# A hand-ordered transformer block: the first part of its order table written anew, with w_phi third on the ACT queue and V of tile 0 between the last folds

## The chip, the core and the metric

The kernel runs on one core of a Trainium2 chip. The core has five engines with an instruction stream each: TensorE (PE, matrix products; its weight loads are shown as PEld), VectorE (DVE), ScalarE (ACT), GpSimd (POOL) and SyncE (SP), which here only issues DMAs. The engines wait for each other through semaphores. An engine takes its instructions strictly in the order in which they are written, so an instruction that waits holds up all that stand behind it. Loads and DMA transposes are issued from SP's queue, and a few loads from ACT's. The metric is the device time of one execution in microseconds, median of the runs. All times in profile rows are counted from the start of the profiled span.

## What is computed

One layer of linear attention with a learned feature map, and after it a gated feed-forward block, over 2048 rows of 640 values in bf16. Cut to what matters:

```python
# A: H = 32 heads of Dh = 20
xn = layernorm(x)
q, k, v = split_heads(xn @ wqkv)                    # wqkv: 640 x 1920
pq, pk = q @ w_phi[h], k @ w_phi[h]                 # w_phi: 32 x 20 x 20
phi(p) = concat(softmax(p), softmax(-p))
kv, z = phi(pk).T @ v, sum(phi(pk))
o = (phi(pq) @ kv) / (phi(pq) @ z + 1e-6)
h = x + o @ wo
# B: F = 1536
hn = layernorm(h)
out = h + ((hn @ w_gate) * (hn @ w_up)) @ w_down
```

## The kernel before

The 2048 rows are 16 tiles t of 128 rows; the 640 values are 5 chunks c of 128. In every name below, the number behind the letters is the tile or the chunk.

Because each head's key is multiplied by w_phi right after the projection, the kernel first folds w_phi into the key and query weights, so that later a single projection gives pk or pq. The steps at the start, with the names that the order table uses and the lines of the profile:

- loads (L285): `x0` ... `x14` are rows of x (one or two tiles each), `w5` is w_phi laid out over partitions (25 KB in runs of 40 bytes), `wk0` to `wk4` are the key weights by chunk, `wv0` to `wv4` the value weights by chunk, 160 KB each.
- `warm0` ... (L367, L372): products of zeros on PE that compute nothing.
- `WTc` (L392): PE transposes chunk c of the key weights; `WTec` (L251) copies the result from PSUM to SBUF. `Ph0` to `Ph2` (L380) spread w_phi into block form.
- `F1_c` (L411): the fold, six products that make chunk c of the folded key weights; `Fe1_c` (L251) copies it into place. `F0_c` and `Fe0_c` do the same for the query weights, whose transposes `wqtc` (L309) are done by DMA straight from HBM. Each `F0_c` reads all five `wqtc`.
- `L1st`, `L1at` (DVE, L428, L429, L431): mean and variance of tile t; `L1lt`, `L1et` (ACT, L436, L439): logarithm and exponential that make 1/sqrt; `L1nt` (L443): the bias for ACT's form; `xnt` (L453 on DVE, L451 on ACT): the normalized tile; `xtt` its transpose, on PE for tiles 0 and 1 (L462, copied by `xtet`), by DMA for the others (L471).
- `Vt`, `Kt`, `Qt` (L482): the projections, ten products of 128x320 each; for tiles 0 and 1 they are five separate steps of two products, one for each chunk, as in `V0_0` to `V0_4`, each of which needs its own chunk's weights only. `Vet` copies V; `Kxt_0`, `Kxt_1` (ACT, L494), `Kst` (DVE, L498), `Krt`, `Ket` (ACT, L501, L503) and `Knt` (POOL, L518) make phi of the keys; `KVt` (L526) adds the tile to kv and z. `Qxt`, `Qst`, `Qrt`, `Qbt` (a subtraction, L563), `Qet`, `Qnt` and the DMA transpose `qTt` (L575) do the like for the queries.
- After that come the division (`Nt`, `ddt`, `ot`), the output projection (`Ot`, L625), the second layernorm, the gated products (`U`, L668) and the last product (`D`, L687).

What sets the order is a table, `PLAN`: one entry for each step, with a key that it is sorted by, the choice among two engines where there is one, and the buffers (PSUM banks and SBUF slots) that it takes:

```python
PLAN[_f[0]] = (float(_f[1]), int(_f[2] or 0) if len(_f) > 2 else 0,
               tuple(int(_v) for _v in _f[3].split(",")) if len(_f) > 3 else ())
```

`arrange` sorts all steps by key and gives each engine its list; `emit` works out the waits. Nothing reorders at run time. So the table is each engine's program order, and the keys have no effect beyond it. The zero products `warm0` to `warm7` stand by dependence ahead of all PE transposes (`wall`).

Of the kernel before, what the change touches and what calls it, by code (L numbers as in the profile page):

```python
# [47 lines left out]
NFILL = 14  # L48
# [189 lines left out]
def build_graph():  # L238
    G = Graph()
# [130 lines left out]
    wm_b = Buf("pwarm", "psum")  # L370
    for k in range(8, 8 + NFILL):
        G.op("pe", "warm%d" % k, lambda e: e.matmul(pb(wm_b)[:, 0:256], lhsT=T["zero"][:, 0:P], rhs=T["zero"][:, :],  # L372
             start=True, stop=True), 0.11, LT, [z_b], [wm_b], -89, before=[G.by["warm%d" % j] for j in range(k)])
    wall = [G.by["warm%d" % k] for k in range(8)]
# [554 lines left out]
```

## Time and profile before

| | us |
|---|---|
| median of 3 runs | 272.42 |
| the three runs | 272.42, 272.93, 272.26 |
| span of the profiled execution, first to last instruction | 270.1 |
| what lies around the span (median less span) | 2.3 |
| PE busy in the span | 264.2 (98%) |
| DVE, ACT, POOL busy | 160.0 (59%), 124.0 (46%), 71.3 (26%) |

The profile page gives no time of its own for the profiled execution beside the span, so the 2.3 us are the median less that span. The busy share is an average over stages with different limits, and PE's products are pipelined, so the question in each stage is which wait ends last before PE can go on. Rows of the timeline give start, length, engine, line and tiles of a group of instructions, and in brackets how long the engine had been idle and what ended it.

### The profile page before, as it was taken

The page shows a single profiled execution, that of the slowest core. Times are in us where ns is not written, and L with a number is a line of the kernel's source. Part 1 is how long each engine was busy: PE and PEld are TensorE (multiplying, and loading weights), DVE is VectorE, ACT ScalarE, POOL GpSimd, SP SyncE. Part 2 cuts the span into 40 slices and gives each one's busy share as a digit, 9 for nine tenths or more (in the row PEclk, how much of TensorE's full clock was granted, in tenths as well). Part 3 has the DMA queues.
Part 4 walks back from the last instruction along what each step waited for, and adds up shares of the span by engine and source line. Part 5 has one row for each costly group of instructions (what it writes and reads, how often), then busy time and mean ns, then how long its engine had stood idle before and what let it go on. Part 6 is the DMA issues. An engine that isn't in the chain of part 4 may idle for free.

```text
span 270.1 us, 5186 instructions
## 1 busy us (share of the span) xinstructions
PE 264.2 (98%) x2092; PEld 177.9 (66%) x2105; DVE 160.0 (59%) x294; ACT 124.0 (46%) x316; POOL 71.3 (26%) x89
## 2 busy tenths in 40 slices
PE   7999999999999999999999999999999999999996
PEld 5777877777777788665556667765554476544774
DVE  4999799978988998577664253332342311423432
ACT  3899999988786382763540051222122300023000
POOL 4255689999923222205000000000000000000000
PEclk9999999999999999999999999999999999999999
DMA  7997995999958897973950001260200001100011
GB/s 200 318 168 136 249 222 129 302 183 245 204 106 143 163 126 149 140 123 64 171 93 2 0 0 36 57 106 1 73 12 2 0 0 51 49 1 0 27 49 61
DMA packets 71752, 28.09 MB, mean 104 GB/s; under 512 B 59056, under 2 KB 71728, under 8 KB 71728
## 3 DMA queue, kind: packets, MB, share of 16 engines
q1 hardware_dynamic: 71168, 27.10, 49.9%
q10 hardware_dynamic: 560, 0.66, 0.8%
q8 instruction: 16, 0.26, 0.4%
q14 instruction: 8, 0.07, 0.1%
HBM read 11.00 MB, written 2.62 MB: 50 GB/s over the span
## 4 chain that ended last, share of the span: by engine, by line
PE 90%; DMA 5%; DVE 2%; ACT 1%; issue 1%; SPq 1%; DVEq 0%
PE ps L668 36%; PE ps L482 24%; PE ps L687 19%; PE ps L625 6%; DMA scratch<-ph 2%; PE ps L526 2%; PE ps L588 2%; DMA Wp<-o 2%; DMA x_all<-in_A_x_dram 1%; PE ps L411 1%; SPq L653 1%; DVE st L428 0%; ACT Wp L251 0%; DVE st L429 0%; DVE ev L676 0%
## 5 line engine op out<-in xcount | busy, mean ns | idle before, releaser
L668 PE MATMUL ps<-xnT,Wgu 128*128 128x512 bf16 (+1 forms) x587 | 106.0, 335 | 0.7
L668 PEld LDWEIGHTS ps<-xnT,Wgu 128*128 128x128 bf16 x600 | 58.3, 98 | 43.4
L673 ACT ACTIVATE gt<-ps 128x512 bf16<-128x512 f32 (+1 forms) x60 | 29.7, 509 | 100.9 <-PE ps L668 62.9
L482 PE MATMUL ps<-Wp,xnT 128*128 128x320 bf16 (+1 forms) x480 | 68.6, 298 | 0.0
L482 PEld LDWEIGHTS ps<-Wp,xnT 128*128 128x128 bf16 x480 | 45.5, 97 | 17.2 <-issue 0.2
L676 DVE TENSOR_TENSOR ev<-ps,gt 128x512 bf16<-128x512 f32 (+1 forms) x60 | 33.6, 579 | 36.5 <-PE ps L668 27.8
L687 PE MATMUL ps<-Wd,ev 128*128 128x320 bf16 (+2 forms) x396 | 53.9, 295 | 0.0
L687 PEld LDWEIGHTS ps<-Wd,ev 128*128 128x128 bf16 x396 | 38.1, 98 | 15.3 <-DVE ev L676 0.2
L699 DVE SCALAR_TENSOR_TENSOR Wp<-ps,rs,x_all 128x640 bf16<-128x640 f32 (+3 forms) x18 | 14.6, 810 | 49.3 <-PE ps L687 49.1
L518 POOL TENSOR_TENSOR ek<-ek,SR 128x1280 bf16<-128x1280 bf16 x16 | 37.5, 2358 | 5.2 <-ACT SR L503 5.1
L551 ACT ACTIVATE ph<-ps 128x600 bf16<-128x600 f32 x32 | 21.4, 680 | 8.0 <-PE ps L482 6.9
L556 DVE TENSOR_REDUCE S<-ph 128x66 f32<-128x1320 bf16 x16 | 23.9, 1516 | 1.8 <-ACT ph L553 1.8
L625 PE MATMUL ps<-Wo,Wp 128*128 128x320 bf16 x160 | 23.9, 299 | 0.2
L498 DVE TENSOR_REDUCE SR<-ek 128x64 f32<-128x1280 bf16 x16 | 23.3, 1468 | 1.0 <-ACT ek L494 1.0
L570 POOL TENSOR_TENSOR ph<-ph,RQ 128x660 bf16<-128x660 bf16 x16 | 20.7, 1308 | 8.9 <-ACT RQ L566 8.9
L646 POOL TENSOR_SCALAR ln<-mv 128x1 f32<-128x1 f32 x12 | 2.3, 191 | 75.7 <-ACT ek L642 75.1
L494 ACT ACTIVATE ek<-ps 128x640 bf16<-128x640 f32 x32 | 21.2, 719 | 2.2 <-PE ps L482 1.5
L625 PEld LDWEIGHTS ps<-Wo,Wp 128*128 128x128 bf16 x160 | 15.3, 98 | 6.4 <-DMA Wp<-o 0.4
L631 DVE SCALAR_TENSOR_TENSOR x_all<-ps,x_all 128x640 bf16<-128x640 f32 x16 | 13.1, 821 | 6.4 <-PE ps L625 6.4
L615 DVE TENSOR_TENSOR o<-ps,sm 128x660 bf16<-128x660 f32 x16 | 13.4, 840 | 0.9 <-ACT sm L608 0.6
L642 ACT ACTIVATE ek<-x_all,mv 128x640 bf16<-128x640 bf16 x16 | 13.1, 821 | 0.0
L251 ACT ACTIVATE ev<-ps 128x640 bf16<-128x640 f32 x16 | 11.2, 704 | 1.1 <-PE ps L482 1.1
(69 smaller groups left out, 161.9 us busy)
## 6 DMA issues: line engine op xcount, KB each, us to landing
out_dram<-Wp SPq DMA_DIRECT2D x15, 160.0 KB, 1.8
Wgu<-in_B_w_gate_dram SPq DMA_DIRECT2D x4, 480.0 KB, 6.2
Wd<-in_B_w_down_dram SPq DMA_DIRECT2D x4, 480.0 KB, 4.7
Wgu<-in_B_w_up_dram SPq DMA_DIRECT2D x4, 480.0 KB, 5.6
x_all<-in_A_x_dram SPq DMA_DIRECT2D x5, 320.0 KB, 5.0
Wp<-in_A_wqkv_dram SPq DMA_DIRECT2D x5, 160.0 KB, 4.7
ev<-in_A_wqkv_dram SPq DMA_DIRECT2D x4, 160.0 KB, 4.2
x_all<-in_A_x_dram SPq DMA_DIRECT2D x3, 160.0 KB, 3.2
```

Of the source, the lines that this page charges most:

```text
L482: ins = e.matmul(pb(b, hb)[:, 0:n1 - n0], lhsT=T["xnT"][:, NC - 1 - c, P * t:P * (t + 1)], rhs=T["Wp"][:, POS[kind], c, n0:n1], start=(c = ...
L494: G.op("act", "%sx%d_%d" % (nm, t, s), lambda e, s=s, b=b, ek=ek: e.activation(out=T["ek"][:, ek.slots[0], 0:2 * D].rearrange("p (b h s f) ...
L498: G.op("dve", "%ss%d" % (nm, t), lambda e, ek=ek, sr=sr: e.tensor_reduce(out=T["SR"][:, sr.slots[0], 0, :], in_=T["ek"][:, ek.slots[0], 0: ...
L518: G.op("pool", "Kn%d" % t, lambda e, eng, ek=ek, sr=sr: e.tensor_tensor(out=T["ek"][:, ek.slots[0], 0:2 * D].rearrange("p (h f) -> p h f", ...
L551: e.activation(out=v[:, 0:10].rearrange("p (b g) j f -> p b g j f", b=2), in_=pp(b, 0, 300).rearrange("p b (g j f) -> p b g j f", j=3, f=D ...
L556: G.op("dve", "Qs%d" % t, lambda e, t=t, ph=ph: e.tensor_reduce(out=T["S"][:, t, 0:66].rearrange("p (g k) -> p g k", k=6), in_=pv(ph).rear ...
L570: return e.tensor_tensor(out=v, in0=v, in1=T["RQ"][:, rq.slots[0], 1, 0:33].rearrange("p (g j) -> p g j", j=3).unsqueeze(3).to_broadcast([ ...
L625: ins = e.matmul(pb(b, hb)[:, 0:320], lhsT=T["oT"][:, oT.slots[0], c, :], rhs=T["Wo"][:, c, 320 * hb:320 * (hb + 1)], start=(c == 0), stop ...
L668: ins = e.matmul(pb(b)[:, 0:n], lhsT=T["Wgu"][:, gu, c, P * ft:P * (ft + 1)], rhs=T["xnT"][:, NC - 1 - c, o0:o0 + n], start=(c == 0), stop ...
L673: G.op("act", "g%d_%d" % (bi, ft), lambda e, pg=pg, gt=gt, n=n: e.activation(out=T["gt"][:, gt.slots[0], 0:n], in_=pb(pg)[:, 0:n], func=AF ...
L676: o_ = G.op("dve", "u%d_%d" % (bi, ft), lambda e, pu=pu, gt=gt, hh=hh, ft=ft, n=n: e.tensor_tensor(out=T["hh"][:, hh.slots[0], ft, 0:n], i ...
L687: ins = e.matmul(pb(b, hb)[:, 0:w], lhsT=T["hh"][:, hh.slots[0], ft, P * tt:P * (tt + 1)], rhs=T["Wd"][:, ft, c0 + w * hb:c0 + w * (hb + 1 ...
```

## The change

The order table is written anew for the first part of the program; from about 75 us on the order is the old one. The keys are whole numbers now, places in the order. The table is 22 lines shorter, so a line L482 of the kernel before is L460 of the changed one, and so for all lines below the table. What it does:

- SP's and ACT's first loads: ACT issues `x0`, `wk1`, `w5` (before: `x1`, `wk3`); SP issues `x1`, `x3`, `wk2`, `wk3`, `wk4`, `wk0`, `x4`, `wv0`, `wv1`, `wv2`, `wv4`, `wv3`, `x2`, `x6`, `x8` (before, with `x0`, `x3`, `w5` ahead: `wk0`, `wk4`, `wk1`, `wk2`, `x4`, `wv1`, `wv0`, `wv2`, `wv3`, `x2`, `wv4`, `x6`). The load `x12` moves from ACT to SP.
- PE: 20 zero products in place of 22, with at least sixteen ahead of any transpose (in the table seventeen, before eighteen); the key weights are transposed in the order 1, 2, 3, 4, 0 and folded in the order 1, 2, 0, 3, 4; `V0_0` to `V0_3` stand between the folds.
- DVE and ACT: DVE takes the statistics of tile 0 first, then `xn0`, `Ph1` (before on POOL), `xn1`; some copies out of PSUM, normalizing steps and bias steps change engine; on POOL the fills of constants come in another order; the subtractions `Qb2`, `Qb4` and `Qb9` move from DVE to POOL.
- SP's DMA transposes between 9 and 27 us come in another order, and `x10` is issued among them.

The few lines of code, with the table's first entries that bear on them:

```diff
-NFILL = 14
+NFILL = 12
...
-    wall = [G.by["warm%d" % k] for k in range(8)]
+    wall = [G.by["warm%d" % k] for k in range(16)]
```

PE's order at the start: before, from the first transpose of the key weights (L392; L372 are zero products, L462 is the transpose of a normalized tile, L411 a fold).

```order
3 L392 MATMUL ps<-ident,ev 128x128 x5
4 L372 MATMUL ps<-ev 128x256 x3
5 L392 MATMUL ps<-ident,ev 128x128 x5
6 L462 MATMUL ps<-ident,xn 128x128 x5
7 L392 MATMUL ps<-ident,ev 128x128 x10
8 L372 MATMUL ps<-ev 128x256
9 L411 MATMUL ps<-Phi,scratch 128x140 x2
```

And in the changed kernel (L370 transposes of the key weights, L350 zero products, L440 transposes of normalized tiles, L389 folds, L460 projections).

```order
3 L370 MATMUL ps<-ident,ev 128x128 x5
4 L350 MATMUL ps<-ev 128x256 x3
5 L370 MATMUL ps<-ident,ev 128x128 x10
6 L440 MATMUL ps<-ident,xn 128x128 x5
7 L370 MATMUL ps<-ident,ev 128x128 x5
8 L440 MATMUL ps<-ident,xn 128x128 x5
9 L389 MATMUL ps<-Phi,scratch 128x140 x2
10 L389 MATMUL ps<-Phi,scratch 128x80 x2
11 L389 MATMUL ps<-Phi,scratch 128x140 x2
12 L370 MATMUL ps<-ident,ev 128x128 x5
13 L460 MATMUL ps<-Wp,xnT 128x320 x2
14 L389 MATMUL ps<-Phi,scratch 128x140 x2
```

Before, two folds ran ahead of the second normalized tile's transpose; now only one fold stands ahead of the first projection step `V0_0` (the L460 row), and both normalized tiles are transposed before the first fold. The other four folds come behind it, with `V0_1` to `V0_3` between them.

SP's queue, before: from the load `x6` to the DMA transposes of tiles 6 and 7 (L471 transposes a normalized tile, L309 a chunk of the query weights).

```order
8 L285 DMA x_all<-in_A_x_dram 128x2x640
9 L471 DMA_TRANSPOSE xnT<-xn 128x5x128
10 L285 DMA x_all<-in_A_x_dram 128x2x640
11 L309 DMA_TRANSPOSE scratch<-in_A_wqkv_dram 128x1x640 x2
12 L471 DMA_TRANSPOSE xnT<-xn 128x5x128
13 L309 DMA_TRANSPOSE scratch<-in_A_wqkv_dram 128x1x640
14 L471 DMA_TRANSPOSE xnT<-xn 128x5x128
15 L309 DMA_TRANSPOSE scratch<-in_A_wqkv_dram 128x1x640
16 L471 DMA_TRANSPOSE xnT<-xn 128x5x128
17 L309 DMA_TRANSPOSE scratch<-in_A_wqkv_dram 128x1x640
18 L471 DMA_TRANSPOSE xnT<-xn 128x5x128 x2
```

And in the changed kernel (L449 transposes a normalized tile, L287 a chunk of the query weights).

```order
6 L263 DMA x_all<-in_A_x_dram 128x2x640 x2
7 L449 DMA_TRANSPOSE xnT<-xn 128x5x128
8 L287 DMA_TRANSPOSE scratch<-in_A_wqkv_dram 128x1x640
9 L263 DMA x_all<-in_A_x_dram 128x2x640
10 L449 DMA_TRANSPOSE xnT<-xn 128x5x128
11 L287 DMA_TRANSPOSE scratch<-in_A_wqkv_dram 128x1x640 x2
12 L449 DMA_TRANSPOSE xnT<-xn 128x5x128
13 L287 DMA_TRANSPOSE scratch<-in_A_wqkv_dram 128x1x640 x2
14 L449 DMA_TRANSPOSE xnT<-xn 128x5x128 x3
15 L263 DMA x_all<-in_A_x_dram 128x2x640 x2
```

The entries are, before: `x6`, `xt3`, `x8`, `wqt4` and `wqt1`, `xt5`, `wqt0`, `xt2`, `wqt2`, `xt4`, `wqt3`, `xt6` and `xt7`; now: `x6` and `x8`, `xt3`, `wqt0`, `x10`, `xt5`, `wqt2` and `wqt3`, `xt2`, `wqt4` and `wqt1`, `xt4`, `xt6` and `xt7`, `x12` and `x14`. Two loads of x share this stretch, all five query-weight transposes stand ahead of `xt4`, and eight transposes follow `xt5`, where seven did.

ACT's list at its start, before (L436 and L439 make 1/sqrt, L251 are copies out of PSUM).

```order
2 L285 DMA x_all<-in_A_x_dram 128x640
3 L285 DMA ev<-in_A_wqkv_dram 128x640
4 L436 ACTIVATE ln<-mv,eps 128x1
5 L439 ACTIVATE rs<-ln 128x1
6 L251 ACTIVATE scratch<-ps 128x5x128
7 L436 ACTIVATE ln<-mv,eps 128x1 x2
8 L439 ACTIVATE rs<-ln 128x1 x2
9 L251 ACTIVATE xnT<-ps 128x5x128
10 L251 ACTIVATE scratch<-ps 128x5x128
11 L251 ACTIVATE Wp<-ps 128x640 x5
```

And in the changed kernel (L414 and L417 make 1/sqrt, L229 are copies out of PSUM).

```order
2 L263 DMA x_all<-in_A_x_dram 128x640
3 L263 DMA ev<-in_A_wqkv_dram 128x640
4 L263 DMA w<-in_A_w_phi_dram 128x5x20
5 L414 ACTIVATE ln<-mv,eps 128x1
6 L417 ACTIVATE rs<-ln 128x1
7 L414 ACTIVATE ln<-mv,eps 128x1
8 L229 ACTIVATE scratch<-ps 128x5x128
9 L417 ACTIVATE rs<-ln 128x1
10 L414 ACTIVATE ln<-mv,eps 128x1
11 L417 ACTIVATE rs<-ln 128x1
12 L229 ACTIVATE scratch<-ps 128x5x128 x2
13 L229 ACTIVATE Wp<-ps 128x640 x4
```

Before, tile 1's logarithm and exponential stood next to each other at the head; now tile 0's come first, and between the logarithm and the exponential of tile 1 stands a copy of transposed key weights (`WTe1`).

More of the change, by code (lines that the diff above doesn't have):

```diff
@@ new lines @@
+id1:21 wk4:22:1 warm8:23::0 warm9:24 glb:25 wk0:26:1 warm10:27 ekz:28 warm11:29 x4:30 warm12:31 L1s0:32 warm13:33 warm14:34 wv0:35:1 warm15:36 warm16:37
+L1a0:38 wv1:39 L1s1:40 WT1:41::3 L1l0:42 warm17:43 wv2:44:1 L1e0:45 warm18:46 warm19:47 L1s3:48 wv4:49:1 wv3:50 Ph2:51 L1a1:52 xn0:53::3 WT2:54::5 x2:55
+L1l1:56 Ph0:57 WTe1:58:1 L1a3:59 WT3:60::0 Ph1:61:1 x6:62 xt0:63::1 L1e1:64 L1l3:65 WT4:66::4 xn1:67::0 x8:68 L1e3:69 WTe4:70 WTe3:71 xt1:72::2 xte0:73:1
+F1_1:74::6 WTe2:75 xte1:76:1 WT0:77::3 Fe1_1:78 WTe0:79:1 V0_0:80::4 F1_2:81::0 L1n3:82:1 xn3:83::2 V0_1:84 Fe1_2:85:1 F1_0:86::2 L1s5:87 xt3:88 V0_2:89
```

158 lines of the change are left out of this document (66 added, 92 removed).

## The prediction

> **What bounds the kernel now.** I read the page first, then the busy time by stage, then the chain of waits, and last the timeline of each engine up to 27 us, where the order changes.
>
> ```profile
> PE 264.2 (98%) x2092; PEld 177.9 (66%) x2105; DVE 160.0 (59%) x294; ACT 124.0 (46%) x316; POOL 71.3 (26%) x89
> ...
> PEclk9999999999999999999999999999999999999999
> ```
>
> ```profile
> 10.50:82.40 71.90, 71.90 (x738) 53.86 (x735) 64.89 (x100) 64.16 (x175) 51.88 (x45) 1.00 0.96 196
> 82.40:130.00 47.60, 46.77 (x408) 33.75 (x407) 38.60 (x79) 25.19 (x72) 12.91 (x20) 1.00 0.82 129
> ```
>
> The columns behind the stretch are its length and the busy time of PE, PEld, DVE, ACT and POOL. From 10.5 us PE has work without a gap for 71.90 us, and in the 47.60 us after it idles 0.83. So two things set the time: how much useful work PE has done when the dense stretch begins, and whether a new wait opens in it. Useful work on PE is the same in both kernels.
>
> ```profile
> 0.83 3.06 DMA x_all<-in_A_x_dram
> ...
> 10.70 14.95 PE ps L482 x110
> 25.65 0.64 PE ps L411 x12
> ```
>
> In the chain of waits the first load of x is what everything waits for, then DVE, ACT and the last fold; from 10.70 it is PE alone. 110 products of a projection take 14.95 us, 0.136 each, so a two-product step such as V0_0 is 0.27.
>
> ```profile
> 1.12 1.89 PE L367 MATMUL ps<-ev 128*128 128x256 bf16 x8 [1.12 <-DVE ev L365]
> ...
> 5.30 0.49 PE L372 MATMUL ps<-ev 128*128 128x256 bf16 x3
> 6.49 0.45 PE L392 MATMUL ps<-ident,ev 128*128 128x128 bf16 x5 [0.70 <-DMA ev<-in_A_wqkv_dram]
> 7.08 0.45 PE L462 MATMUL ps<-ident,xn 128*128 128x128 bf16 x5
> 7.37 0.72 PE L392 MATMUL ps<-ident,ev 128*128 128x128 bf16 x10
> 7.93 0.27 PE L372 MATMUL ps<-ev 128*128 128x256 bf16 x1
> 8.04 0.80 PE L411 MATMUL ps<-Phi,scratch 128*128 128x140 bf16 x12
> 8.68 0.44 PE L392 MATMUL ps<-ident,ev 128*128 128x128 bf16 x5
> 8.95 0.44 PE L462 MATMUL ps<-ident,xn 128*128 128x128 bf16 x5
> ...
> 10.54 15.11 PE L482 MATMUL ps<-Wp,xnT 128*128 128x320 bf16 x110
> ```
>
> PE's timeline gives the steps, start to start: a transpose of a tile 0.29 (7.08 to 7.37), a fold 0.32 (two from 8.04 to 8.68), a transpose of weights 0.27 (8.68 to 8.95). At 10.54 all five weight transposes, both tile transposes and five folds are behind PE.
>
> **The new start, step by step.** The second tile's transpose now stands ahead of every fold, so the question is when xn1 is there.
>
> ```profile
> 3.91 0.49 DVE L428 BATCH_NORM_STATS2 st<-x_all 128x6 f32<-128x320 bf16 x1 [2.85 <-DMA x_all<-in_A_x_dram]
> ...
> 5.50 0.19 DVE L431 BATCH_NORM_AGGREGATE mv<-st 128x2 f32<-128x12 f32 x1
> 5.61 0.44 DVE L428 BATCH_NORM_STATS2 st<-x_all 128x6 f32<-128x320 bf16 x1
> ...
> 6.47 0.55 DVE L453 TENSOR_SCALAR xn<-x_all,mv,rs 128x640 bf16<-128x640 bf16 x1
> ...
> 7.05 0.44 DVE L251 COPY scratch<-ps 128x640 bf16<-128x640 bf16 x1
> 7.59 0.61 DVE L453 TENSOR_SCALAR xn<-x_all,mv,rs 128x640 bf16<-128x640 bf16 x1
> ```
>
> ```profile
> 5.73 0.29 ACT L436 ACTIVATE ln<-mv,eps 128x1 f32<-128x1 f32 x1 [3.65 <-DVE mv L431]
> 6.06 0.20 ACT L439 ACTIVATE rs<-ln 128x1 f32<-128x1 f32 x1
> 6.17 0.69 ACT L251 ACTIVATE scratch<-ps 128x640 bf16<-128x640 bf16 x1
> 6.75 0.72 ACT L436 ACTIVATE ln<-mv,eps 128x1 f32<-128x1 f32 x2
> ```
>
> x0 is now ACT's first load, as x1 was, so DVE starts at 3.91 again. A tile's statistics take 0.80 (3.91 to 5.50 is two), an aggregate 0.11 (5.50 to 5.61). The new order has tile 0, aggregate, tiles 1 and 3, aggregate: tile 1's begins at 3.91 + 3 x 0.80 + 0.11 = 6.42. Its logarithm follows 0.23 behind (5.50 to 5.73), at 6.65. Behind it on ACT now stands a weight copy, and only then the exponential. The copy can start some 0.2 later (my estimate; one that waits for the logarithm starts after 0.33, 5.73 to 6.06), holds ACT for 0.58 (6.17 to 6.75), and the exponential takes 0.20: 7.63. The subtraction takes 0.61, to 8.27; PE follows 0.06 later (7.02 to 7.08), at 8.33. Tile 0's products are then long done, and Ph1 on DVE fits into the wait.
>
> From 8.33 PE goes through transpose, fold F1_1 and transpose WT0: 8.33 + 0.29 + 0.32 + 0.27 = 9.21. V0_0 also needs wv0.
>
> ```profile
> 4.65 1.90 SPq L285 DMA_DIRECT2D Wp<-in_A_wqkv_dram  x4
> ...
> 9.14 1.31 SPq L471 DMA_TRANSPOSE xnT<-xn  x1
> ...
> 11.11 3.44 SPq L309 DMA_TRANSPOSE scratch<-in_A_wqkv_dram  x2
> 14.59 1.28 SPq L471 DMA_TRANSPOSE xnT<-xn  x1
> ...
> 21.17 1.27 SPq L309 DMA_TRANSPOSE scratch<-in_A_wqkv_dram  x1
> 22.49 2.60 SPq L471 DMA_TRANSPOSE xnT<-xn  x2
> ```
>
> In the view of DMA issues, with the us from issue to landing, w_phi and the first value load stand so:
>
> ```profile
> w<-in_A_w_phi_dram SPq DMA_DIRECT2D x1, 25.0 KB, 4.3
> ...
> Wp<-in_A_wqkv_dram SPq DMA_DIRECT2D x1, 160.0 KB, 4.8
> ```
>
> The first value load, issued at 4.65, lands 4.8 later, at 9.45. It was wv1; now wv0 has that place, with the same loads ahead of it on the two queues together, so V0_0 starts at 9.5. Four V steps (1.09) and the other four folds (1.28) bring PE to 11.87, where the kernel before would stand at 10.54 + 1.09 = 11.63. **Term 1: +0.25.** Without the wait for wv0 it would be -0.05.
>
> V0_1 to V0_3 need the next value loads, half a microsecond apart (four issues in 1.90), and come at steps of about 0.6, wv3 with a place later: margins of 0.1 to 0.4, where before V began 2 us behind its loads. One place later costs 0.47. **Term 2: +0.1**, between 0 and 0.6.
>
> **The query folds.** 94 projection products follow, 94 x 0.136 = 12.78: F0_2's turn is at 11.97 + 12.78 = 24.75. It needs all five query-weight transposes; the last of them is now the sixth of a row that starts with tile 5's. That place was 14.59 to 21.17 before, 6.58 for five issues.
>
> Four of SP's transposes, each alone in its stretch of the view of DMA issues, with the us from issue to landing: tile 3's (issued at 9.14), a query chunk's (21.17), the one issued right behind tile 5's, and tile 4's.
>
> ```profile
> xnT<-xn SPq DMA_TRANSPOSE x1, 5.5
> ...
> scratch<-in_A_wqkv_dram SPq DMA_TRANSPOSE x1, 3.2
> ...
> scratch<-in_A_wqkv_dram SPq DMA_TRANSPOSE x1, 5.0
> ...
> xnT<-xn SPq DMA_TRANSPOSE x1, 2.8
> ```
>
> When does tile 5's come? WTe0 starts 0.56 behind WT0 (6.49 to 7.05), so at 9.50, and with xn3 behind it (0.44, a bias step, 0.60) tile 3's transpose is issued at 10.8, not 9.14. Behind it a query-weight transpose (1.27, or 2.17 where it was the second of the 3.44) and x10 (about 0.6): 14.1 to 15.0. I take 14.8. The last query transpose is issued at 21.4 and lands 3.2 later, 24.6, just in time; tile 4's, now behind it, lands at 22.7 + 2.8 = 25.5, where V4's turn is 24.75 + 0.64 = 25.4; V6 is as close. Before, tile 4's was issued one place ahead of the last query transpose, at 21.17 - 1.31 = 19.86. The margins are gone: 0 at best, and with a landing of 5.0, which one of the five had, 1.7. Nearest is the low end, with x10's 320 KB in line as well. **Term 3: +0.5.**
>
> The rest costs nothing: the two zero products fall in PE's idle time (0.70 at 6.49); the three subtractions go to POOL, which has 20 us free in the dense stretch (71.90 - 51.88); x12 comes later, as x10 did before, for which DVE waited 1.3 us (the second of the two below) while PE stayed dense. ACT begins the key features later, but it has 7.7 us free in that stretch (71.90 - 64.16); if these don't suffice, PE waits for PSUM.
>
> ```profile
> DVE st L428 <- DMA x_all<-in_A_x_dram: 4.2, 2, 2.9
> ```
>
> Sum: +0.85, span 270.1 + 0.85 = 270.9, and with the 2.3 around it, which make the span the median of 272.4: **273.3 us.**
>
> **The clock.** The profile shows the full clock in all 40 slices. Yet the first eight zero products took 0.24 each, those at 5.30 0.16. From the end of these at 5.8 PE ran only transposes until 7.93; now it does until the first fold at 8.62, 2.8 us against 2.1. [...]
>
> **Rivals.**
> 1. *Not slower.* PE's V steps fill the waits: wv0 lands early (-0.05), tile 5's transpose at 14.1, and the 0.83 us of idle time behind 82 us takes up part of what is left. Time 272.0 to 272.7. For it: every term is small. Against: xn1 is reached through DVE and ACT alone, so earlier loads of weights gain 0.3 at most. Faster by 0.8 would need nearly all the idle time that PE has from 10.5 to 130 us.
> 2. *SP's transposes come late.* Term 3 at its high end: F0_2 waits 1.7, and V4 and V6 behind it; 272.4 + 0.25 + 0.1 + 2 = 274.8. For it: tile 3's transpose took 5.5 to land and one query transpose 5.0. Against: the 5.0 ran beside x12 on ACT's queue, which is gone there.
> 3. *w_phi on ACT's queue lands late*, so that the change does not bring it early at all: Ph1 stands ahead of xn1 on DVE, so past 7.3 us each microsecond is paid in full. At 8.3: 274.3. Before, as third on SP's queue (issues about half a microsecond apart from 0.8) and 4.3 from issue to landing, it was there at about 6; third on ACT's that leaves 1.3.
> [...]
>
> **How the numbers follow.** A measurement of this kernel tells about 0.3%, 0.8 us, from no change (its runs differ by 0.67). My forecast, 272.9 to 274.0: 0.47. Rival 1: 0.24; rival 2: 0.14; rival 3: 0.08; rival 4: 0.04; something else 0.03. Slower by over 0.3% is above 273.24: 0.28 of the forecast's 0.47 and rivals 2 to 4, together 0.54. Faster needs the low end of rival 1: 0.07. Within: 0.39. The range of 8 in 10, with rival 1's middle and rival 2: 272.2 to 275.0.
>
> **What would show it.** Right: xn1's transpose on PE near 8.3, the 94 products from near 11.9, PE idle before L389 or L460 near 25 us with a DMA transpose as releaser. Wrong: PE's first V step well ahead of 9.5 (term 1), no wait at 25 (term 3), or a wait at 30 to 75 us for ACT or POOL, which would be the features' late start.

## The result

| | us |
|---|---|
| before, median of 6 runs | 272.41 |
| changed, median of 6 runs (274.60 to 276.92) | 275.45 |
| ratio, 95% interval | 1.0122 (1.0097 to 1.0147) |
| spans of the two profiled executions | 270.1 and 273.3 |

The changed kernel is slower by 1.2%, 3.0 us, where 0.85 was predicted. A second measurement of the same kernel, against the kernel before beside it, gave 1.0103 (1.0072 to 1.0133).

### The profile page after: what moved, and what is told of

It reads as the page before. It is cut to its first block, busy times and chain, and to the rows that moved or that the text cites. A ratio compares the mean times of both kernels' runs of the same rounds, so it can differ in the third digit from the quotient of the medians.

```text
span 273.3 us, 5182 instructions
## 1 busy us (share of the span) xinstructions
PE 265.4 (97%) x2090; PEld 177.9 (65%) x2103; DVE 159.1 (58%) x296; ACT 122.5 (45%) x314; POOL 71.0 (26%) x89
## 4 chain that ended last, share of the span: by engine, by line
PE 75%; DVE 10%; DMA 8%; ACT 4%; POOL 1%; issue 1%; SPq 0%; DVEq 0%
PE ps L646 36%; PE ps L665 19%; PE ps L460 10%; PE ps L603 7%; DMA Wp<-o 3%; DMA x_all<-in_A_x_dram 3%; DVE SR L476 2%; DVE st L407 2%; DMA xnT<-xn 2%; PE ps L566 2%; DVE st L406 2%; DVE xn L431 2%; ACT ek L472 1%; PE ps L504 1%; POOL ek L496 1%; ACT ph L529 1%
## 5 line engine op out<-in xcount | busy, mean ns | idle before, releaser
L460 PE MATMUL ps<-Wp,xnT 128*128 128x320 bf16 (+1 forms) x480 | 69.1, 299 | 0.9 <-DMA xnT<-xn 0.9
L460 PEld LDWEIGHTS ps<-Wp,xnT 128*128 128x128 bf16 x480 | 45.2, 97 | 18.6 <-DMA xnT<-xn 1.4
L677 DVE SCALAR_TENSOR_TENSOR Wp<-ps,rs,x_all 128x640 bf16<-128x640 f32 (+3 forms) x18 | 14.6, 810 | 49.3 <-PE ps L665 49.1
L603 PE MATMUL ps<-Wo,Wp 128*128 128x320 bf16 x160 | 23.9, 299 | 1.6 <-DMA Wp<-o 1.5
L603 PEld LDWEIGHTS ps<-Wo,Wp 128*128 128x128 bf16 x160 | 15.2, 98 | 8.3 <-DMA Wp<-o 2.4
L229 ACT ACTIVATE ev<-ps 128x640 bf16<-128x640 f32 x14 | 9.8, 706 | 2.3 <-PE ps L460 2.2
```

Of the source, the lines that this page charges most:

```text
L460: ins = e.matmul(pb(b, hb)[:, 0:n1 - n0], lhsT=T["xnT"][:, NC - 1 - c, P * t:P * (t + 1)], rhs=T["Wp"][:, POS[kind], c, n0:n1], start=(c = ...
L603: ins = e.matmul(pb(b, hb)[:, 0:320], lhsT=T["oT"][:, oT.slots[0], c, :], rhs=T["Wo"][:, c, 320 * hb:320 * (hb + 1)], start=(c == 0), stop ...
```

## The profile after

First the page of the changed kernel, then its windows with the boundaries of before (length, then busy time of PE, PEld, DVE, ACT, POOL, the granted clock, the DMA share, GB/s).

```profile
PE 265.4 (97%) x2090; PEld 177.9 (65%) x2103; DVE 159.1 (58%) x296; ACT 122.5 (45%) x314; POOL 71.0 (26%) x89
...
q8 instruction: 16, 0.26, 0.4%
```

```profile
10.50:82.40 71.90, 70.64 (x717) 52.56 (x715) 62.13 (x98) 62.16 (x168) 52.78 (x48) 1.00 0.88 189
82.40:130.00 47.60, 45.82 (x418) 33.14 (x419) 38.65 (x77) 26.22 (x76) 12.49 (x19) 1.00 0.76 127
```

The dense stretch is dense no longer: PE idles 1.26 us in it (71.90 less 70.64) where it idled nothing, and 1.78 behind it where it idled 0.83. The clock is 1.00 in both. Where the idle time lies, PE's timeline of the changed kernel shows (L440 is the transpose of a normalized tile, L389 a fold, L460 a projection, L504 the products of KV, L566 those of N, L603 those of O).

```profile
8.60 0.46 PE L440 MATMUL ps<-ident,xn 128*128 128x128 bf16 x5 [0.45 <-DVE xn L431]
...
9.21 0.44 PE L370 MATMUL ps<-ident,ev 128*128 128x128 bf16 x5
9.64 0.43 PE L460 MATMUL ps<-Wp,xnT 128*128 128x320 bf16 x2
...
11.73 12.99 PE L460 MATMUL ps<-Wp,xnT 128*128 128x320 bf16 x94
25.08 0.80 PE L389 MATMUL ps<-Phi,scratch 128*128 128x140 bf16 x12 [0.36 <-issue]
...
46.87 0.49 PE L504 MATMUL ps<-ev,ek 128*128 128x63 bf16 x11
...
47.75 6.41 PE L460 MATMUL ps<-Wp,xnT 128*128 128x300 bf16 x46
55.07 4.26 PE L460 MATMUL ps<-Wp,xnT 128*128 128x320 bf16 x30 [0.90 <-DMA xnT<-xn]
59.17 0.49 PE L504 MATMUL ps<-ev,ek 128*128 128x63 bf16 x11
...
114.84 0.50 PE L566 MATMUL ps<-KVm,scratch 128*128 128x63 bf16 x11
...
118.20 2.89 PE L603 MATMUL ps<-Wo,Wp 128*128 128x320 bf16 x20 [1.22 <-DMA Wp<-o]
```

The rows of PE's timeline before that stand for the same steps: KV7, KV8 and N15.

```profile
45.80 0.49 PE L526 MATMUL ps<-ev,ek 128*128 128x63 bf16 x11
...
57.02 0.49 PE L526 MATMUL ps<-ev,ek 128*128 128x63 bf16 x11
...
113.00 0.51 PE L588 MATMUL ps<-KVm,scratch 128*128 128x63 bf16 x11 [0.44 <-DMA scratch<-ph]
```

Step against step, PE is 1.07 us late at KV7 (46.87 less 45.80): the start. At KV8 it is 2.15 late; between the two lies V13, which waits for a DMA transpose of a normalized tile. At N15 it is 1.84 late, since the wait that the kernel before has there (0.44) is gone. Then O6 waits 1.22, and the span ends 3.2 later. So there are three places: the start, V13 and O6. (The steps ahead of KV7, KV8, N15 and O6 on PE are the same ones in both kernels, only in another order, so the rows compare equal work.)

The prediction looked at the first. For the second, SP's timeline of the changed kernel (L449 is a tile's transpose, L263 a load, L553 a query tile's transpose) and DVE's around it:

```profile
42.58 1.20 SPq L449 DMA_TRANSPOSE xnT<-xn  x1
43.82 2.32 SPq L263 DMA_DIRECT2D Wgu<-in_B_w_up_dram  x4
50.17 1.20 SPq L449 DMA_TRANSPOSE xnT<-xn  x1
```

```profile
48.15 1.48 DVE L476 TENSOR_REDUCE SR<-ek 128x64 f32<-128x1280 bf16 x1
49.55 0.60 DVE L431 TENSOR_SCALAR xn<-x_all,mv,rs 128x640 bf16<-128x640 bf16 x1
```

and SP's of the kernel before:

```profile
42.15 3.84 SPq L471 DMA_TRANSPOSE xnT<-xn  x3
46.04 2.30 SPq L285 DMA_DIRECT2D Wgu<-in_B_w_up_dram  x4
```

The transpose at 50.17 is tile 13's, `xt13`. Before, it was the first of the three at 42.15, ahead of the four 480 KB loads `wu2`, `wu3`, `wu0`, `wu1`. The new table puts `xn13` behind `Ks11` on DVE (the two DVE rows), so it ends 8 us later, and `xt13` behind the four loads. The chain of waits of the changed kernel has both late waits as pieces (start, length):

```profile
50.17 4.85 DMA xnT<-xn
...
113.52 4.64 DMA Wp<-o
```

## Tile 13: six runs

The question is whether tile 13's place causes the second loss, and by what: the loads ahead of its transpose (theory A) or the late subtraction by itself (rival D). The entries are a name, its key, and slots; nothing else of the table is touched.

**Both put back early** (in the changed kernel):

```diff
-xn13:338::3  xt13:341
+xn13:290.5::3  xt13:296.5
```

> The changed kernel, with only tile 13's subtraction (xn13) and its transpose (xt13) put back to the place that they have in the kernel before: xn13 ahead of xn15 on DVE, xt13 ahead of xt15 on SP. Theory A (queue): the changed kernel's second loss, 1.3 us at V13 (55.07 us), comes from xt13 standing behind four 480 KB loads, and PE's lateness then passes through SP's row of transposes (77 to 125 us) to the end, the wait of 1.22 at O6 with it. Then V13 doesn't wait, PE is about 1 us later than in the kernel before from 40 us to the end, and the time is 273.3 to 273.8. Rival B: the wait at O6 has a cause of its own (oT6 took 4.6 us to land, 3.8 before) and stays: 274.2 to 274.6. Rival C: what is gained at V13 is lost at the next wait, since something else sets the end: 275.2 to 275.6.

Measured: ratio 1.0051 (1.0027 to 1.0075), 273.36 us against 271.80 beside it. PE's timeline of this run has no wait from KV7 to KV8:

```profile
47.40 11.04 PE L460 MATMUL ps<-Wp,xnT 128*128 128x300 bf16 x80
58.28 0.50 PE L504 MATMUL ps<-ev,ek 128*128 128x63 bf16 x11
```

Neither V13 nor O6 waits; the span is 1.0 longer than before's. A's number came, B's and C's did not: about half of the loss goes with this one tile.

**Only the subtraction early**, twice (`xn13:290.5`, `xt13` still behind the loads):

> The changed kernel, with only the subtraction xn13 put back early (ahead of xn15 on DVE); its transpose xt13 stays behind the four loads on SP. Theory A (queue): xt13 is issued at about 46.2, right behind wu1, but lands only behind it (52.4), at 53.7 to 55.0; V13 waits 0.1 to 1.4; time 274.0 to 275.5. Rival D (late subtraction): xt13 lands 2.6 to 3 us from its issue, at about 49, V13 doesn't wait, time 273.3 to 273.8.

> The kernel with only xn13 early, a second time: xt13 still behind the four loads on SP. Is its time (ratio 1.0036) a matter of xn13's place, or of the one profiled execution in which the instruction fetch came 0.1 us after xt13's packets? If of xn13's place: xt13 lands again about 0.7 us behind wu1, V13 waits under 0.4, ratio 1.003 to 1.007. If of the fetch's chance: the fetch hits wu1 or xt13 this time, xt13 lands 1.5 to 2 us later against wu0's landing (4 in place of 2.1), V13 waits 0.5 to 1.5, and the ratio lies towards 1.010.

Measured: ratios 1.0036 (1.0014 to 1.0057) and 1.0065 (1.0038 to 1.0092); no wait at V13 in either profile, though `xt13` took 6.9 and 6.8 us from issue to landing behind the loads (SP's timeline of the first, where the issue itself took 2.96 us, and the row in its view of DMA issues):

```profile
47.48 2.96 SPq L449 DMA_TRANSPOSE xnT<-xn  x1
```

```profile
xnT<-xn SPq DMA_TRANSPOSE x1, 6.9
```

So where `xt13` stands in SP's queue need not matter; when `xn13` is done does. In both profiles PE came late from the start (1.9 and 2.6 us at KV7), which helps to hide it.

**One place earlier**, ahead of `Ks11` (`xn13:330.5`), with a start as late as the changed kernel's:

> The changed kernel with xn13 one place earlier on DVE, ahead of Ks11 in place of behind it (1.5 us): xt13 is issued at 48.5 to 48.8, not 50.1, and stands behind the four loads on SP, whose last lands at 52.4 to 54.3. If it is enough that xt13 is issued before the loads are through (it moves right behind them): V13 waits 0 to 0.6, ratio 1.004 to 1.008. If the subtraction must come 8 us earlier: V13 waits 0.9 to 1.8 as in the changed kernel, ratio 1.009 to 1.013.

Measured: ratio 1.0044 (1.0019 to 1.0069). SP's and PE's timelines:

```profile
48.65 1.20 SPq L449 DMA_TRANSPOSE xnT<-xn  x1
```

```profile
47.07 11.05 PE L460 MATMUL ps<-Wp,xnT 128*128 128x300 bf16 x80
57.95 0.50 PE L504 MATMUL ps<-ev,ek 128*128 128x63 bf16 x11
```

`xt13` is issued 1.52 us earlier, lands 4.3 later, at 53.0, and V13 doesn't wait: one place on DVE is enough.

**The loads behind xt13** (the changed kernel; `xn13` late):

```diff
-wu2:303 wu3:304 wu0:309 wu1:316
+wu2:341.1 wu3:341.2 wu0:341.3 wu1:341.4
```

> The changed kernel, with the four loads wu2, wu3, wu0, wu1 put behind xt13 on SP's queue; the subtraction xn13 stays late, behind Ks11. Theory A (queue): xt13 is issued at 50.2 as in the changed kernel, but lands about 2.6 later, at 52.8, ahead of V13's turn at 53.6; no wait there, time 273.3 to 273.8, as with xn13 and xt13 both early. Rival D (late subtraction): that xn13 ends at 50.15 rather than 42.1 is enough by itself; xt13 lands near 55 again, V13 waits some 1.3, time 275.2 to 275.6.

Measured: ratio 1.0281 (1.0235 to 1.0328); both theories missed the time. PE's and SP's timelines, and the transpose in the view of DMA issues:

```profile
54.33 4.26 PE L460 MATMUL ps<-Wp,xnT 128*128 128x320 bf16 x30 [0.49 <-DMA xnT<-xn]
```

```profile
51.10 3.44 SPq L263 DMA_DIRECT2D Wgu<-in_B_w_up_dram  x4
54.58 4.63 SPq L553 DMA_TRANSPOSE scratch<-ph  x1
```

```profile
q8 instruction: 1, 0.02, 3.4%
...
xnT<-xn SPq DMA_TRANSPOSE x1, 4.4
```

With no load ahead of it `xt13` still takes 4.4 us, and V13 still waits (PE loses 0.67 between KV7 and KV8). So A, as a story of the queue alone, falls. One rival is left open here: the four loads are issued at 51.10, right behind `xt13`, and move beside it. The time is worse for another reason: `qT1`, now behind the loads, lands 7.4 us after its issue, the next query tile waits for its buffer, and PE idles 3.0 us ahead of 65.01. And in five of the six runs the mean granted clock was 0.988 to 0.994, not 1.00 as in the profiled one, which is the fastest (277.08 of a median of 279.77).

**The converse**, the kernel before with `xn13` behind `Ks11` and `xt13` behind `wu1`:

> The converse: the kernel before, with xn13 moved behind Ks11 on DVE and xt13 behind wu1 on SP, as they stand in the changed kernel. Theory A (queue): in the kernel before the last of the four loads lands at 56.15; with xt13 out of the row ahead of them at about 55; xt13 lands 1.3 to 2.6 behind, at 56.3 to 57.6, and V13, whose turn is 52.8, waits 3.5 to 4.8. Nothing gives it back: 275.9 to 277.2. Rival D (late subtraction): xn13 ends near 48.6, xt13 lands at 51 to 52, no wait, 272.2 to 272.7. Rival C (another thing sets the end): a wait at V13, but less than 1 us of it left at the end, under 273.4.

Measured: ratio 1.0105 (1.0064 to 1.0145). PE's timeline:

```profile
55.73 4.26 PE L482 MATMUL ps<-Wp,xnT 128*128 128x320 bf16 x30 [2.07 <-DMA xnT<-xn]
```

The wait appears in the old kernel too, 2.24 us between KV7 and KV8, and stays to the end (the span is 2.6 longer). A had its place right and its size too high; D expected no wait and C no lasting loss, and fell.

The table gives, for each profile, how late the rows of KV7, KV8 and N15 start against those of the kernel before, and the span against 270.1.

| kernel | KV7 | KV8 | gained between | N15 | span |
|---|---|---|---|---|---|
| changed | 1.07 | 2.15 | 1.08 | 1.84 | 3.2 |
| changed, second profile | 0.74 | 2.49 | 1.75 | 2.52 | 3.2 |
| before, tile 13 late | 0.57 | 2.81 | 2.24 | 2.65 | 2.6 |
| loads behind | 0.74 | 1.41 | 0.67 | 4.28 | 5.3 |
| both early | 1.26 | 1.26 | 0 | 1.07 | 1.0 |
| subtraction early | 1.89 | 1.90 | 0 | 1.29 | 1.2 |
| subtraction early, again | 2.57 | 2.57 | 0 | 2.44 | 3.2 |
| one place earlier | 0.93 | 0.93 | 0 | 0.11 | 0.1 |

In all seven profiles with `xn13` late (three more below) PE loses 0.67 to 2.33 us between the two rows. (In the one with 2.33, `oT6` one place earlier, 0.60 of it is a wait for ACT at V9.) In all nine profiles of a changed kernel with `xn13` earlier it loses nothing.

## The instruction fetch: two runs

Why does a transpose that takes 2.6 us elsewhere (`xt15`, 42.58, in the same trace) take 4.4 to 5.3 at this place? The DMA view of the changed kernel for 52.0 to 54.5 (40 slices; then the queues, with packets, MB and their share of 16 engines):

```profile
GB/s 217 406 98 156 254 75 16 0 0 0 0 0 0 0 0 131 0 0 0 0 8 8 57 123 193 201 209 221 176 188 160 90 45 25 184 156 20 8 12 8
...
q14 instruction: 1, 0.01, 3.0%
q8 instruction: 1, 0.02, 2.9%
```

For about 0.8 us, from 52.45 to 53.25, no data packet starts. What is there are two instruction fetches: the one on queue 8 takes 2.9% of 16 engines over 2.5 us, 1.16 us of one engine. Sixteen of them come in a span (the page), one for about 260 of PE's 4193 instructions; that they bring PE's code was the author's guess from this ratio. That gave theory E, and two runs: the changed kernel once more, and one meant to move the fetches by 24 more narrow zero products at the start, which PE has idle time for (its first sixteen are narrower, too):

```diff
-NFILL = 12
+NFILL = 36
+WN = lambda k: 128 if k < 16 else 64 if k < 40 else 256
```

> The changed kernel, unchanged, on the chip of the next three. Theory E, formed from the traces so far: V13's wait is made by an instruction fetch (16 KB on queue 8, which comes at 52 to 54 us in every trace, with another of 8 KB on queue 14 near it) that holds one of the 16 DMA engines for 1.1 us just when the packets of xt13's transpose are moved; that happens because xn13 is done, and xt13 issued, 8 us later than before. The fetch goes with PE's place in its program, so V13 waits again, 0.9 to 1.5 us, and the time is 1.0% to 1.4% above the kernel before. Rival F (chance): the 4.9 us that xt13 took to land are an accident of the one profiled execution; this profile shows no wait at V13 and a span near 272.

> The changed kernel with 24 more zero products on PE (48 of PE's instructions, 64 columns each; the first 16 are cut to 128 columns, so that all end before the first weights land). Nothing else moves; only every later fetch of PE's code comes 48 instructions earlier in the work, some 2 to 3 us, at 49 to 50.5 us in place of 52.1. Theory E: xt13, issued at about 50.2 as in the changed kernel, is through behind the last of the four loads (52.4) at 53.0 to 53.4, ahead of V13's turn; V13's wait falls from 1.3 us to under 0.3. The time follows by as much, 273.4 to 274.3, unless another transpose is hit by the moved fetch. Rival A (queue: only the loads ahead of it make xt13 late) and rival D (only the late subtraction does): nothing in these is touched, xt13 lands near 55 again and V13 waits 0.9 to 1.5; 274.9 to 275.7.

Measured: the changed kernel again 1.0103; V13 waits again (PE loses 1.75; `xt13` 5.3 us), so F, chance, falls. With the moved fetches 1.0102 (1.0079 to 1.0125), and V13 waits still, 0.87. But the fetch there came at 52.6, no earlier at all, so this run doesn't answer what it was made for. Elsewhere the fetches did move, from 28.2 to 25.7 and from 115.5 to 113.2 among them, and there are seventeen, so they follow PE's program. The waits moved with them: O6 doesn't wait now, and V6 does (PE's timeline, and the DMA view for 25.7 to 26.8):

```profile
27.92 1.53 PE L461 MATMUL ps<-Wp,xnT 128*128 128x320 bf16 x10 [1.36 <-DMA xnT<-xn]
```

```profile
GB/s 94 633 19 9 0 0 0 0 0 0 0 0 0 0 0 0 0 0 65 93 112 149 177 214 205 158 214 214 186 484 195 205 186 186 205 140 158 149 121 74
...
q8 instruction: 1, 0.02, 5.4%
```

V6 needs `xt6`, issued at 23.6. It took 4.24 us to land here, with the fetch 2.1 behind its issue, and 2.65 in both profiles of the changed kernel, where the fetch came 4.0 behind. So `xt6` here and `xt13` in the changed kernel, with a fetch 2.1 and 1.9 us behind their issue, took 4.24 and 4.85 us, against 2.65 for `xt6` and 2.6 for `xt15` with none so near, and who waits changed with where the fetch fell: V6 in this run, O6 in the changed kernel.

How much of `xt13`'s 4.85 us is the fetch no run separates, but the profiles allow an estimate. In the three in which `xn13` alone is earlier, `xt13` lands 0.6 to 0.7 us behind the last of the four loads (54.33 behind 53.66, 54.98 behind 54.30, 52.96 behind 52.36). In the changed kernel that load lands at 52.39; by the same step `xt13` would have landed near 53.0, ahead of V13's turn at 54.16, and it landed at 55.03. By this estimate the lateness of `xn13` puts the transpose in the fetch's way, and the fetch makes the wait.

## The start: five runs

**The three subtractions.** Tile 13 early, and `Qb2`, `Qb4`, `Qb9` back on DVE (flag `:1`):

> Tile 13 early, as in the first experiment, and the three subtractions Qb2, Qb4 and Qb9 back on DVE. The prediction costed their move to POOL at nothing: the same time as the first experiment, 273.1 to 273.6. Rival: POOL's row of subtractions holds back the query features between 57 and 72 us, and the time falls by 0.3 us or more, below 273.0.

Measured: 1.0060 (1.0035 to 1.0086), against 1.0051 (1.0027 to 1.0075) without the edit: no difference that these intervals can tell, as costed.

**The row of query weights.** Tile 13 early, and SP's row changed in two ways (the first line with + is the first trial, the second the second):

```diff
-xt3 wqt0 x10 xt5 wqt2 wqt3 xt2 wqt4 wqt1 xt4 xt6 xt7 x12
+xt3 wqt0 xt5 wqt2 xt2 wqt3 wqt4 wqt1 xt4 x10 xt6 xt7 x12
...
+xt3 wqt0 wqt2 xt5 wqt3 xt2 wqt4 wqt1 xt4 xt6 xt7 x10 x12
```

> Tile 13 early, as in the first experiment, and beside it the SP order of the start: x10 moved from behind wqt0 to behind xt4, xt2 moved ahead of wqt3, and on DVE the statistics of tiles 10 and 11 behind Ks5 and Ve4, since their data comes later. The prediction's term 3 (and the wait of V2 for xt2, which it didn't have): all query transposes come about 0.6 earlier, PE's waits at V2 (0.2), F0_2 (0.65) and V4 (0.1) go, and PE is 0.1 to 0.4 later than in the kernel before at 40 us: 272.3 to 272.8. Rival (the start costs something else, at xn1 and the V steps): PE is still about 1 us later at 40 us, 273.3 to 273.8.

> Tile 13 early, as in the first experiment, and SP's row at the start set so that x10's load no longer stands among the transposes: wqt2 ahead of xt5, xt2 ahead of wqt3, x10 behind xt7, with the statistics of tiles 10 and 11 behind Ks2. (In the trial before this, x10 stood ahead of xt6, which then landed 2.4 us late.) The prediction's term 3: the last query transpose is issued at about 20.8, not 21.5, and lands at 24.1 to 24.5; F0_2 waits 0 to 0.2 where it waited 0.65, V2 not at all, V4 not at all. PE is 0.2 to 0.6 later than in the kernel before at 40 us; ratio 1.001 to 1.003 (1.0051 with tile 13 early alone). Rival: the start's loss lies in the xn1 chain and the V steps, ahead of 12 us; PE is still 0.9 or more later at 40 us, ratio 1.004 to 1.006.

Measured: 1.0133 (1.0094 to 1.0172) and 1.0132 (1.0093 to 1.0171), slower than with tile 13 alone. PE's timeline of the first, then of the second:

```profile
25.14 0.80 PE L389 MATMUL ps<-Phi,scratch 128*128 128x140 bf16 x12 [0.69 <-issue]
...
29.05 1.53 PE L460 MATMUL ps<-Wp,xnT 128*128 128x320 bf16 x10 [1.76 <-DMA xnT<-xn]
```

```profile
24.57 0.80 PE L389 MATMUL ps<-Phi,scratch 128*128 128x140 bf16 x12
...
34.07 1.86 PE L460 MATMUL ps<-Wp,xnT 128*128 128x320 bf16 x10 [2.28 <-DVE ev L229]
```

In the first, SP still waits for `xn5` (`xt5` issued at 14.53, 14.99 in the changed kernel), so moving `x10` gains nothing, and `xt6` behind it is late. In the second the wait at the query folds is gone (no bracket, 24.57 for 25.08), but `x10` now lands at 31.4, DVE waits 1.9 us for it, and V7 waits for DVE. Behind that wait the granted clock is 0.51 from 35.1 to 38.6, in this profiled run alone of the six, which costs PE more than a microsecond again there.

**x10's work moved too.** The same row, with the statistics of tiles 10 and 11 later on DVE and their logarithm later on ACT; once with tile 13 early, once late:

> Tile 13 early, and SP's row at the start as in the run of the row of query weights (wqt2 ahead of xt5, xt2 ahead of wqt3, x10 behind xt7); the statistics of tiles 10 and 11 now stand behind Ve6 on DVE and their logarithm behind Ke2 on ACT, since x10 lands only at 31.4 and DVE, waiting for it, held back Ve6 and with it V7 (2.4 us) in that run. Theory T (term 3): what the start costs is the late row of query-weight transposes and nothing else of size; PE is 0.2 to 0.6 us later than in the kernel before at 40 us, and with tile 13 early nothing else is lost: ratio 1.000 to 1.004. Rival U: x10's 320 KB have no place in the changed order that costs nothing, or the lateness comes back in SP's row behind 77 us: ratio 1.005 or more.

> The same repair of the start, but tile 13 late as in the changed kernel. If the start and tile 13 are two separate losses: V13's turn comes 0.5 to 0.8 us earlier than in the changed kernel while xt13 lands near 55 again, V13 waits 1.8 to 2.4 us, and the ratio is 1.006 to 1.010, 0.5% to 0.8% above the run beside it. Rival V (one thing: the lateness of the start makes V13 wait): V13's wait goes, the ratio is that of the run beside it.

Measured: 1.0129 (1.0096 to 1.0163) and 1.0177 (1.0138 to 1.0217). In the first V5 waits 0.51 us for `xt5` at 19.58, so this row has no fixed gain either. The second shows the start at its best, and what it costs (PE's timeline):

```profile
24.29 0.80 PE L389 MATMUL ps<-Phi,scratch 128*128 128x140 bf16 x12
...
27.96 0.50 PE L504 MATMUL ps<-ev,ek 128*128 128x63 bf16 x11
...
34.04 1.53 PE L460 MATMUL ps<-Wp,xnT 128*128 128x320 bf16 x10 [0.84 <-ACT ek L472]
```

No wait for the query weights is left, and KV0 comes at 27.96; in the two profiles of the changed kernel it comes 0.3 and 0.9 later. Then the logarithm for tiles 10 and 11, waiting on ACT for DVE (1.5 us in two waits), holds the key features behind it, and at KV7 PE is 1.75 late. T, with 1.004 at most, missed. U holds: in none of three trials did `x10` find a place that costs nothing. The intervals of 1.0177 and 1.0129 overlap, so the times alone don't show that tile 13 is a loss of its own; the profiles do: PE loses 1.18 at V13 with tile 13 late and nothing with it early, on the same start. V, one cause for both, falls.

## The late stretch: three runs

**oT6 ahead of oT13** in the changed kernel (`oT13:641` to `oT13:649.5`), **all three repairs together**, and **the kernel before with qT15 ahead of hT5** (`qT15:105.972` to `qT15:104.6`):

> The changed kernel, with oT6 one place earlier in SP's row of transposes, ahead of oT13 (O6 stands ahead of O13 on PE). Theory G: PE's second late wait, 1.1 to 1.2 us at O6, is SP's row of back-to-back transposes, 3 us later than in the kernel before, with the instruction fetch at 115.5 us on top; one place is 1.5 us, so oT6 lands at about 115 to 116.7, O6 waits under 0.2, and since O13 has 3 us of margin nothing else waits: 1.1 to 1.5 us less than the changed kernel (whose ratio to before was 1.0122 and 1.0103), a ratio of 1.005 to 1.008. Rival H: O6's wait is only one of several that the late SP row makes, and the next one takes it over: ratio 1.009 to 1.013 as without the edit.

> All three repairs on the changed kernel: tile 13 early, SP's row at the start as in the run before this one, oT6 ahead of oT13. If each of the three losses is one of its own, what is left is the start's 0.2 to 0.6 us: ratio 0.999 to 1.003, no difference that can be told from the kernel before. If SP's row between 77 and 125 us or the fetches set the end by themselves, ratio 1.004 or more.

> The kernel before, with qT15 one place earlier on SP, ahead of hT5. In the kernel before PE waits about 0.5 us for qT15 at N15 (113 us), and every later kernel gives back up to 0.77 us of its lateness there. If that wait is its own, it goes to 0 to 0.2 and the time falls by 0.2 to 0.5 us: ratio 0.998 to 0.9995. Rival: hT5, one place later, lands at 110.3 and U1_1_0 waits for it in its place: ratio 1.000 or more.

Measured: 1.0101 (1.0061 to 1.0141), 1.0117 (1.0081 to 1.0154) and 1.0000 (0.9980 to 1.0020). PE's timeline of the first:

```profile
118.85 1.52 PE L603 MATMUL ps<-Wo,Wp 128*128 128x320 bf16 x10
121.20 1.53 PE L603 MATMUL ps<-Wo,Wp 128*128 128x320 bf16 x10 [0.83 <-DVE o L593]
```

O6, at 118.85, waits no more, and O13 behind it does: rival H. The run with all repairs has `x10`'s wait (1.9 us at V7, and 3.4 us at half clock behind it) and O13's. In the third, N15 no longer waits (its row has no bracket), and the time is that of the kernel before.

What goes with O6's wait shows when all 18 profiles of this study are laid side by side. In seven of them `oT6` takes 4.2 to 4.6 us to land and O6 waits (the changed kernel twice, loads behind, subtraction early again, subtractions on DVE, and both with `x10`'s work moved), and in each of the seven a fetch on queue 8 comes 1.3 to 2.4 us behind the issue of `oT6`. In the others it comes within 0.6 us of the issue or 2.3 and more behind it, `oT6` takes 2.7 to 3.8, and O6 never waits. The upper border isn't sharp: 2.37 in one that waits, 2.33 in one that doesn't. Being late alone doesn't do it: the first trial of the row of query weights is 2.9 late at KV8 and has no wait at O6. This is a pattern over profiles, not an experiment of its own.

No run beat the kernel before. The nearest of the changed kernels are those with tile 13 moved and nothing else: 1.0051, 1.0036 and 1.0065 (one kernel, twice) and 1.0044.

## Why the prediction was wrong

- **"The rest costs nothing": this step failed.** It went through the subtractions, `x12` and the late features on ACT, and no cost of these was found. It did not compare DVE's and SP's lists behind 27 us, so it put at nothing what it had not looked at: `xn13` eight us later and `xt13` behind four loads. That cost 1.1 and 1.75 us at V13 in the two profiles, and about half of the time by the runs. The slack could have been estimated from the trace before: `Ks11` starts at 47.33 on DVE and takes 1.40 to the next start, so `xn13` behind it would end near 49.3, and V13's turn is at 52.9 (46.14 and 50 products of 0.136). That is 3.6 us, for a transpose that takes 2.6 us alone and 2.8 to 5.5 in the rows that the prediction itself quoted. In the changed kernel it was 4.0 (50.15 to 54.16), and `xt13` took 4.85.
- **Direction: right. Size: 0.85 us for 3.0, outside the range.** The forecast's sum is about right for the start alone (1.07 and 0.74 late at KV7 in the two profiles of the changed kernel), and the start is somewhat under half of the loss.
- **Term 1 (+0.25): right in kind.** The working counts V0_3 twice, in the four V steps and in the 94 products that follow; only three V steps stand ahead of the row of 94. Against equal work in the kernel before (10.54 and three steps of 0.27: 11.35), that row is 0.38 late in the first profile (11.73) and 0.10 in the second (11.45). The slip also puts F0_2's turn 0.27 too late (24.48, not 24.75), and 7.63 + 0.61 is 8.24, not 8.27. `xt1` came at 8.60 and at 8.31, predicted 8.33. What delayed V0_0 (9.64) was not wv0, which was issued at 4.09, where the working has 4.65, and landed at 8.69, not 9.45.
- **Term 2 (+0.1): nothing.** In the two profiles of the changed kernel the V steps between the folds have no wait.
- **Term 3 (+0.5): right.** The last query transpose lands at 24.99, and F0_2 follows at 25.08 (the profile names no releaser for its wait). From the row of 94 to V4 behind the two folds PE loses 0.68 in the first profile and 0.35 in the second, 0.5 on average over the nine with this start; in the four profiles with the row of query weights repaired it lost 0.05 or nothing in two, 0.5 and 0.7 in the two others.
- **The start as a whole.** Over the nine profiles with this start PE is 0.74 to 2.57 late at KV7, 1.4 on average, where three with the old start have -0.12 to 0.57. So it costs some 1.2. What the sum lacks are a late w_phi (rival 3) and a stretch at half clock (rival 4), which came in some executions.
- **"A wait at 30 to 75 us for ACT or POOL" was named as what would prove it wrong.** The wait came in that stretch, but for a DMA.
- **What comes of a late PE.** The prediction took every term as final. N15 gives back up to 0.8 us (0.93 late at KV8 became 0.11), while O6 took 1.2 more in the profiled run of the changed kernel, in which a fetch came 1.97 us behind the issue of `oT6`.
- **Rivals 1 and 2.** 1 (not slower) fell with the start's 1.2. 2 (SP's transposes late) was the right kind at the wrong place: F0_2 and V4 lost 0.3 to 0.7 in the two profiles, not 1.7 and more.
- **Rival 3 (w_phi late on ACT's queue) came in four of the nine profiles with this start.** In the two of the changed kernel w_phi landed at 5.79 and 6.20, ahead of `Ph1`'s turn, and `Ph2` started on POOL as it landed (the first row, of the first profile). But in four others (both early; subtraction early, twice; `oT6` earlier) it landed at 7.60 to 8.48, and DVE waited 0.5 to 1.3 us for it at `Ph1`, ahead of `xn1` (the second row, of the second run with the subtraction early). At the row of 94 products these four are 0.48 to 2.58 late, the other five 0.10 to 0.44. None of their edits touches the first 40 us, so this differs from execution to execution; how many of the timed runs had it is not known.

```profile
5.87 1.27 POOL L358 TENSOR_TENSOR Phi<-w,GL 128x280 bf16<-128x280 bf16 x2 [2.41 <-DMA w<-in_A_w_phi_dram]
```

```profile
8.50 0.33 DVE L358 TENSOR_TENSOR Phi<-w,GL 128x160 bf16<-128x160 bf16 x1 [1.31 <-DMA w<-in_A_w_phi_dram]
```

- **Rival 4 (half clock, 0.04 of the chances) came in one of them.** The 0.54 for a slower kernel takes in its 0.04; no run shows what makes PE slow, and half clock stands in one of the nine profiles with this start. In the changed kernel it fell: the granted clock was 1.00 in every window and 0.999 or more in all twelve runs, and a V step and a fold took 0.27 and 0.32 (9.64 to 9.91 to 10.23), as before, behind 2.5 us of transposes (6.34 to 8.88). But in the run just shown, the one with w_phi at 8.48, PE ran nothing but transposes from 6.06 to 10.01, the granted clock was 0.50 from 9.2 to 12.6, and a fold took 0.58 there, a V step 0.53. Its page shows this in the second slice:

```profile
PEclk9799999999999999999999999999999999999999
```

## What to carry to other kernels

When a table of orders is written anew, compare the whole list of every engine, not the part that the change is named for. For each step that a transfer waits on, set the time from its end to the first use against the slowest such transfer in the trace, not the usual one. And judge a rival by all profiles that share the stretch it speaks of: one profile showed neither the late w_phi nor the half clock. A load taken out of a tight row of transfers must go somewhere, and its consumers with it: three repairs of the start moved the wait without removing it.

## What the runs showed of the hardware

A fetch (16 KB on queue 8, one packet, 16 in a span) takes 0.9 to 1.4 us of one DMA engine in the profiles of the kernel before and of the changed one, and DMA transposes issued shortly ahead of it landed late: in the changed kernel the five issued 1.3 to 2.0 us ahead took 4.2 to 4.9 us, and `xt15`, issued 9.5 ahead, 2.6. The changed kernel started no data packet for 0.8 us at 52.45, the run with moved fetches none for 0.4 at 25.8, and the transposes under way took 4.85 and 4.24 us to land. The fetch's packet at 52.1 takes 1.18 us, to 53.27, and data packets start again at 53.25. How the packet holds the transpose up is not shown; that the two share a DMA engine is the author's estimate from these times.

The same order gave starts that differ by 1.8 us from one profile to the next (0.74 to 2.57 at KV7). With them differed the landing of w_phi, 25 KB in runs of 40 bytes, issued at 1.74 each time: 5.79 to 8.48.

A stretch at half clock (granted 0.50 from 9.2 to 12.6, 0.51 from 35.1 to 38.6) lasted 3.4 us in each of the three profiles that have one. It came where PE had had long waits: 2.1 us of them between 6.3 and 9.4 us in one, and the 2.3 and 1.9 us at V7 in the two others. Not every such wait brings one: the 3.0 us in the profile with the loads behind did not. One such stretch makes a mean granted clock of 0.994 over a run of 273 us (half of 3.4 us lost), and single runs of several of these kernels show just that.
